# Fused linear attention and SwiGLU block on one core: fewer waits at the end, a last block in three pieces, and a reordered head

## The chip, the cores and the metric

One core of one Trainium2 chip. The metric is device time in microseconds (us) of one execution. The profiled executions have a span about 1.8 us below the time of the same run, so spans are compared with spans and times with times.

## The reference, cut to what matters

```python
def reference(A_x, A_wqkv, A_wo, B_x, B_w_gate, B_w_up, B_w_down):   # x: 1 x 2048 x 1024, F = 3584
    x = A_x
    xn = _layernorm(x, axis=-1)
    s = _A_ref(xn, A_wqkv, A_wo)             # linear attention, 32 heads, phi(t) = elu(t) + 1
    g = _silu(_B_ref(xn, B_w_gate, B_w_up, B_w_down))   # SwiGLU feed-forward, then silu
    return x + s * g
```

Everything starts from layer-normed x, so the first products need x tiles (128 tokens x 1024), their normalisation, their transposes, and the first blocks of `wqkv`. The last thing computed is a block of the down projection, which then goes through silu, a multiply, a transpose, the residual add and a store.

## The kernel before

The kernel builds a list of operations with data dependencies, runs a list scheduler 24 times with estimated durations, keeps the best order, and emits one fixed instruction stream for each engine with semaphore waits between them. The products use Strassen-Winograd sums. Four parts matter.

The waits. Each emitted operation knows what its engine has already waited for, directly or through others (`ek`):

```python
    def emit(self, esem):
        ...
            for p in sorted(o.preds, key=lambda p: -pos[p]):
                ...
                sem, key, val, ek = p.ev
                if kn.get(key, 0) >= val:
                    continue
                prog[o.eng].append(("w", sem, val))
                for k, v in ek.items():
                    if kn.get(k, 0) < v:
                        kn[k] = v
        ...
        self.count = count
...
        prog = PL.emit(esem)
        for s in semn.values():                       # at the end: SyncE waits for every DMA semaphore
            if id(s) in PL.count:
                prog["sp"].append(("w", s, PL.count[id(s)]))
```

The warm-up, the loads and the normalisation of the head (NWARM = 14):

```python
        dve([], [wz_r], lambda h: h.memset(wz, 0.0), 256)
        for n in range(NWARM):
            b = n % 8
            pe_mm([ident_r, wz_r], [bank_r[b]], [(ps[b][:, :], ident[:, :], wz, True, True)])
...
        def x_load(i):
            ...
            if i:
                dma([], [s.r], s.ap(), xf[i * 128:(i + 1) * 128, :], dsem("x%d" % s.k), 256 * KB).urgent = 10.0
                return
            for h, e in enumerate(("sp", "act")):     # tile 0 in two halves, on SyncE's and ScalarE's queue
                ...
        def wkv_load(w, j, k):                        # one block of wqkv, 512 KB
            ...
        for n, (fn, args) in enumerate(((x_load, (0,)), (wkv_load, (0, 1, 0)), (x_load, (1,)), (wkv_load, (0, 1, 1)),
                                        (wkv_load, (0, 0, 0)), (wkv_load, (0, 0, 1)), (x_load, (2,)),
        ...
        ln_tile(0)
        t_tile(0)          # transposes of tile 0 on TensorE
        ln_tile(1)
        p_piece(0, 0, 1)   # products of tile 0 with blocks 1 and 2
        p_piece(0, 0, 0)   # products of tile 0 with blocks 3 and 4
        t_tile(1)
        p_piece(1, 0, 1)
        ...
```

The end of the last down block: 14 pairs of products for each half of 256 tokens, then silu, multiply, transposes, add, and a store of 128 KB; between them the 256 KB store of an earlier block (`self.turn0`):

```python
                for h, b in enumerate((self.sets[1].b, self.b2)):
                    for n in range(0, NPAIR, 2):
                        ...
                        if turns and n == 2:
                            self.turn0()
                        if turns and n == 8:
                            turn(turns.pop())
                    ... # Silu, multiply
                    turns.append(h)
                turn(1)
```

## Time and profile before

| | before |
|---|---|
| time, median of 3 runs | 718.42 us (717.95 to 718.52) |
| span of the profiled execution | 716.4 us |
| TensorE busy | 99% of the span |
| first product at the steady rate (13th product) | 11.34 us |
| fourth block of wqkv landed | 11.29 us |
| last store issued, landed | 712.35, 714.35 us |

PE is TensorE, DVE is VectorE, ACT is ScalarE, SP is SyncE; L275 is the line of the helper that issues matmuls, L418 that of a tensor-tensor helper, so go by the tiles. First the top of the profile's page, which gives span and busy time of each engine:

```profile
span 716.4 us, 11259 instructions
PE 706.9 (99%) x4114; PEld 389.3 (54%) x4128; DVE 641.5 (90%) x1530; ACT 405.1 (57%) x777; POOL 12.4 (2%) x35
```

Next the view by windows: for each stretch its length, then the busy time of each engine, the clock granted to TensorE (1.00 is full), the DMA share and GB/s.

```profile
6.36:11.34 4.98, 4.19 (x29) 1.91 (x29) 3.69 (x9) 2.00 (x6) 0.55 (x1) 1.00 1.07 367
11.34:711.00 699.66, 697.51 (x4070) 385.37 (x4084) 634.66 (x1513) 401.50 (x771) 8.30 (x14) 1.00 0.48 135
...
714.40:716.50 2.10, 0.00 (x0) 0.00 (x0) 0.00 (x0) 0.00 (x0) 0.00 (x0) 0.72 0.02 4
```

From 11.34 to 711 us TensorE is busy 697.5 of 699.7 us: only the ends can give time. In the last 2.1 us no engine computes anything.

The head in TensorE's timeline (start, length from first start to last end, then the group; in brackets the idle time before it and what ended it):

```profile
7.11 1.04 PE L275 MATMUL ps<-H,X 128*128 128x512 bf16 x4
8.45 1.02 PE L275 MATMUL ps<-H,X 128*128 128x512 bf16 x4 [0.30 <-DMA H<-in_A_wqkv_dram]
9.85 1.04 PE L275 MATMUL ps<-H,X 128*128 128x512 bf16 x4 [0.38 <-DMA H<-in_A_wqkv_dram]
10.73 0.61 PE L282 MATMUL ps<-ident,W 128*128 128x128 f16 x8
11.34 1.69 PE L275 MATMUL ps<-H,X 128*128 128x512 bf16 x7
```

Three groups of four products with blocks 1, 2 and 3. The first waits for the evacuated transposes of tile 0 (block 1 had landed at 4.92); the second and third begin as their block lands (8.31 and 9.81). Then come the eight transposes of tile 1, and then the 13th product, the first with block 4. The 13th product starts at 11.34, right behind the transposes. But a load is done when all 16 of its parts have landed, and in the trace's record of landings the last part of block 4 comes at 11.29 (the first at 9.85). The transposes are hidden in a wait for a load.

The same stretch on VectorE (tile 1's variance, a sum of weights, tile 1's normalise):

```profile
8.02 0.15 DVE L740 TENSOR_SCALAR veps<-mv 128x1 f32<-128x1 f32 x1
8.34 0.69 DVE L418 TENSOR_TENSOR H<-H 128x1024 f16<-128x1024 bf16 x1 [0.16 <-DMA H<-in_A_wqkv_dram]
8.95 0.73 DVE L750 TENSOR_SCALAR W<-W,mv,rstd 128x512 f16<-128x512 bf16 x2
```

The tail: SyncE's semaphore waits at the end (by source line: count, length in ns, first and last start).

```profile
L267 SPq EVENT_SEMAPHORE  x48: 28/28/28, 712.8 to 716.0; - x48
```

And SyncE's timeline, where L421 is the helper that issues DMAs:

```profile
707.18 5.54 SPq L421 DMA_DIRECT2D out_dram<-TM  x5
```

48 closing waits, each for two semaphores, run at one per 0.06 us (a count of 49, as in the prediction, includes one of the barrier that follows). The five stores were issued at 707.18 (256 KB), 710.19 (256), 710.82 (128), 711.24 (256) and 712.35 (128); the last landed at 714.35.

### The profile page before, as it was taken

What the parts mean: (1) busy time and instruction counts of PE and PEld (TensorE: products, weight loads), DVE (VectorE), ACT (ScalarE), POOL (GpSimd) and SP (SyncE); (2) the same over time, 40 slices, a digit from 0 to 9 for tenths busy, and PEclk for the clock granted to TensorE, in tenths of its full rate; (3) what the DMA queues carried; (4) which work ended last, traced back from release to release, by engine and by line L of the source; (5) the groups of instructions that cost most, each with busy time, mean ns of one, the idle gap of its engine ahead of it and who ended that gap; (6) DMA issues with size and microseconds to landing.
All of it is one profiled execution on the core that took longest, in us unless ns stands there. A gap on an engine that the chain in (4) does not pass through costs nothing.

```text
span 716.4 us, 11259 instructions
## 1 busy us (share of the span) xinstructions
PE 706.9 (99%) x4114; PEld 389.3 (54%) x4128; DVE 641.5 (90%) x1530; ACT 405.1 (57%) x777; POOL 12.4 (2%) x35
## 2 busy tenths in 40 slices
PE   8999999999999999999999999999999999999997
PEld 3544445555555555555556455555555555565653
DVE  7999988989999999998957999999999999797852
ACT  3677644887679565664212157766876756521111
POOL 2111000000000000000000000000000000000000
PEclk9999999999999999999999999999999999999999
DMA  9426235245464343326496954132716241747653
GB/s 307 104 60 131 47 117 177 67 146 186 153 188 128 111 155 110 112 64 179 133 198 171 269 155 133 60 118 93 205 59 192 74 147 64 197 115 171 138 157 86
DMA packets 138743, 98.12 MB, mean 137 GB/s; under 512 B 32832, under 2 KB 135744, under 8 KB 138688
## 3 DMA queue, kind: packets, MB, share of 16 engines
q1 hardware_dynamic: 138544, 97.28, 47.7%
q8 instruction: 32, 0.52, 0.3%
q10 hardware_dynamic: 144, 0.13, 0.1%
q14 instruction: 23, 0.19, 0.1%
HBM read 77.59 MB, written 12.71 MB: 126 GB/s over the span
## 4 chain that ended last, share of the span: by engine, by line
PE 94%; DVE 3%; DMA 1%; ACT 1%; issue 0%; SPq 0%; DVEq 0%
PE ps L275 94%; DMA H<-in_A_wqkv_dram 1%; DVE W L418 1%; DVE H L418 1%; DVE ps L418 1%; ACT TM L407 0%; PE ps L282 0%; DVE P L418 0%; DVE TM L418 0%; SPq L421 0%; DVE H L811 0%; ACT ps L407 0%; ACT H L407 0%; DVE TM L810 0%; SPq L717 0%
## 5 line engine op out<-in xcount | busy, mean ns | idle before, releaser
L275 PE MATMUL ps<-X,W 128*128 128x512 f16 (+1 forms) x1358 | 289.1, 352 | 0.7 <-DVE W L418 0.6
L407 ACT ACTIVATE TM<-ps 128x512 f16<-128x512 f32 (+2 forms) x354 | 186.6, 549 | 109.1 <-PE ps L275 106.8
L275 PE MATMUL ps<-H,W 128*128 128x512 f16 (+2 forms) x1090 | 218.8, 351 | 0.9 <-DVE ps L418 0.4
L418 DVE TENSOR_TENSOR W<-W 128x1024 f16<-128x1024 bf16 (+5 forms) x416 | 186.2, 482 | 5.4 <-PE ps L275 4.7
L275 PEld LDWEIGHTS ps<-X,W 128*128 128x128 f16 (+1 forms) x1358 | 132.1, 98 | 105.1 <-DVE W L418 1.1
L275 PEld LDWEIGHTS ps<-H,W 128*128 128x128 f16 (+1 forms) x1096 | 105.6, 98 | 95.0 <-DVE ps L418 1.5
L418 DVE TENSOR_TENSOR ps<-ps,TM 128x256 f32<-128x256 f32 (+1 forms) x250 | 131.3, 528 | 13.3 <-PE ps L275 10.9
L407 ACT ACTIVATE ps<-ps 128x512 f32<-128x512 f32 (+1 forms) x173 | 85.0, 492 | 100.1 <-PE ps L275 98.3
L275 PE MATMUL ps<-P,W 128*128 128x256 f16 (+1 forms) x516 | 99.5, 319 | 0.0
L407 ACT ACTIVATE H<-ps 128x512 f16<-128x512 f32 (+1 forms) x126 | 75.1, 605 | 41.5 <-PE ps L275 41.3
L418 DVE TENSOR_TENSOR H<-H 128x1024 f16<-128x1024 f16 (+5 forms) x126 | 70.7, 579 | 0.6 <-ACT H L407 0.2
L275 PEld LDWEIGHTS ps<-P,W 128*128 128x128 f16 (+1 forms) x516 | 50.2, 98 | 29.5 <-DVE ps L418 0.7
L407 ACT ACTIVATE TM<-TM 128x512 f16<-128x512 f32 (+1 forms) x61 | 38.0, 622 | 47.0 <-DVE TM L418 46.8
L275 PE MATMUL ps<-W 128*128 128x256 f16 (+1 forms) x330 | 62.0, 282 | 0.2
L418 DVE TENSOR_TENSOR TM<-ps,TM 128x512 f32<-128x512 f32 (+2 forms) x62 | 41.5, 670 | 13.5 <-PE ps L275 12.4
L418 DVE TENSOR_TENSOR H<-H,TM 128x512 f16<-128x512 f16 x112 | 45.5, 418 | 8.9 <-ACT H L407 8.7
L275 PEld LDWEIGHTS ps<-W 128*128 128x128 f16 (+1 forms) x330 | 31.6, 98 | 32.5 <-DVE ps L418 1.3
L275 PE MATMUL ps<-H,X 128*128 128x512 bf16 (+1 forms) x147 | 35.0, 379 | 0.9 <-DMA H<-in_A_wqkv_dram 0.7
L275 PE MATMUL ps<-H,P 128*128 128x512 bf16 (+1 forms) x108 | 26.4, 379 | 0.1
L418 DVE TENSOR_TENSOR H<-ps,TM 128x512 f16<-128x512 f32 (+1 forms) x35 | 24.0, 686 | 1.9 <-PE ps L275 1.5
L275 PEld LDWEIGHTS ps<-H,X 128*128 128x128 f16 (+1 forms) x150 | 14.0, 98 | 17.9 <-ACT X L407 1.2
L418 DVE TENSOR_TENSOR TM<-TM,W 128x512 f16<-128x512 f16 (+1 forms) x39 | 14.1, 365 | 10.5 <-ACT TM L407 10.5
(96 smaller groups left out, 430.2 us busy)
## 6 DMA issues: line engine op xcount, KB each, us to landing
W<-in_B_w_gate_dram SPq DMA_DIRECT2D x14, 1024.0 KB, 5.1
W<-in_B_w_up_dram SPq DMA_DIRECT2D x13, 1024.0 KB, 5.5
W<-in_B_w_down_dram SPq DMA_DIRECT2D x14, 896.0 KB, 6.4
H<-in_A_wqkv_dram SPq DMA_DIRECT2D x8, 512.0 KB, 8.1
H<-r_scratch SPq DMA_DIRECT2D x32, 128.0 KB, 3.7
W<-m_scratch SPq DMA_DIRECT2D x4, 1024.0 KB, 5.1
s_scratch<-TM SPq DMA_DIRECT2D x32, 128.0 KB, 2.6
TM<-in_A_x_dram SPq DMA_DIRECT2D x16, 256.0 KB, 3.2
```

The lines of the kernel that those rows point to most:

```text
L275: last = h.matmul(o, l, r, start=st, stop=sp, skip_group_check=True)
L407: q = PL.op("act", reads, writes, lambda h: h.activation(o, i, func, **kw), nel(o) / (1000.0 if "bias" in kw or not isinstance(kw.get("sca ...
L418: return dve(reads, writes, lambda h: h.tensor_tensor(o, a, b, op), nel(o), 1.92 if fast else 0.96)
```

## The change

The intent: await at the end only the DMAs that SyncE does not already know to be complete; shorten the closing chain by cutting the last block into pieces of 256, 128 and 128 tokens, the last stored from ScalarE's queue; start the warm-up of TensorE earlier and with fewer full-size products; and load x tiles 0 and 1 ahead of all weights, so that tile 1 is normalised sooner.

```diff
@@ emit
-        self.count = count
+        for o in (o for o in self.order if o.sem is not None):
+            sem, key, val, _ = o.ev
+            if val == count[key] and know["sp"].get(key, 0) < val:
+                prog["sp"].append(("w", sem, val))
@@ warm-up (NWARM 14 -> 15)
-        wz_r = TM.reg(0, 1 * KB)
-        dve([], [wz_r], lambda h: h.memset(wz, 0.0), 256)
+        wz_r = [TM.reg(0, KB // 4), TM.reg(KB // 4, 3 * KB // 4)]
+        dve([], [wz_r[0]], lambda h: h.memset(wz[:, 0:128], 0.0), 64)
+        dve([], [wz_r[1]], lambda h: h.memset(wz[:, 128:512], 0.0), 192)
         for n in range(NWARM):
             b = n % 8
-            pe_mm([ident_r, wz_r], [bank_r[b]], [(ps[b][:, :], ident[:, :], wz, True, True)])
+            m = 512 if n > 3 else 128
+            pe_mm(wz_r[:1 + n // 4], [bank_r[b]], [(ps[b][:, 0:m], wz[:, 0:128], wz[:, 0:m], True, True)])
@@ ln_tile: tile 1's second statistics half now waits for tile 0's last normalise
             if i == 1:
-                for o in (oA, oB):
-                    o.preds.add(first_var[0])
-                    first_var[0].succs.append(o)
+                for o, q in zip((oA, oB), first):
+                    o.preds.add(q)
+                    q.succs.append(o)
@@ loads
-        for n, (fn, args) in enumerate(((x_load, (0,)), (wkv_load, (0, 1, 0)), (x_load, (1,)), (wkv_load, (0, 1, 1)),
+        for n, (fn, args) in enumerate(((x_load, (0,)), (x_load, (1,)), (wkv_load, (0, 1, 0)), (wkv_load, (0, 1, 1)),
@@ last down block
+                        self.last = [(0, 256, b), (256, 128, balloc()), (384, 128, balloc())]
...
+                    PL.op("act" if h == 2 else "sp", [vr], [], lambda h: h.dma_start(dst, v), 0.47,
+                          sem=dsem("oz%d" % h), nbytes=512 * n)
...                                     # the loop over two halves becomes a loop over self.last
-                        if turns and n == 2:
+                        if h == 1 and n == 2:
                             self.turn0()
-                        if turns and n == 8:
+                        if turns and n == (4 if h == 2 else 10):
                             turn(turns.pop())
...
-                turn(1)
+                for h in reversed(turns):
+                    turn(h)
@@ end of build_kernel
         prog = PL.emit(esem)
-        for s in semn.values():
-            if id(s) in PL.count:
-                prog["sp"].append(("w", s, PL.count[id(s)]))
```

More of the change, by code (lines that the diff above doesn't have):

```diff
@@ L283, in _tr_group, with build_kernel @@
     return last
-def build_kernel(nc, A_x, A_wqkv, A_wo, B_w_gate, B_w_up, B_w_down, out, WINDOW=6, NWARM=14, NPE=4, LEAD=12.0):
+def build_kernel(nc, A_x, A_wqkv, A_wo, B_w_gate, B_w_up, B_w_down, out, WINDOW=6, NWARM=15, NPE=4, LEAD=12.0):
     S, D, FF = 2048, 1024, 3584
@@ L725, in build_kernel @@
         xnslot = {}
-        first_var = []
+        first = []
         def ln_tile(i):
@@ L741, in ln_tile @@
             if i == 0:
-                first_var.append(o0)
+                first.append(o0)
             pool([ver, nh_r], [rsr], lambda h: h.tensor_tensor(rstd[:, j, :], veps[:, j, :], neg_half[:, :], ALU.pow), 0.56)
@@ L749, in ln_tile @@
                 for c in range(0, 1024, n):
-                    dve([s.r, mvr, rsr], [o.sub(2 * c, 2 * n).r], lambda h, c=c: h.tensor_scalar(
+                    o0 = dve([s.r, mvr, rsr], [o.sub(2 * c, 2 * n).r], lambda h, c=c: h.tensor_scalar(
                         oa[:, c:c + n], xa[:, c:c + n], mv[:, j, 0:1], rstd[:, j, :], ALU.subtract, ALU.mult), n, 2.6)
+                if i == 0:
+                    first.append(o0)
             else:
@@ L1462, in do @@
                         b = self.sets[1].b
-                        self.b2 = balloc()
-                        act([bank_r[b]], [bank_r[self.b2], bank_r[b]], ps[self.b2][:, 0:256], ps[b][:, 256:512], ACT.Identity)
+                        self.last = [(0, 256, b), (256, 128, balloc()), (384, 128, balloc())]
+                        for o, n, q in self.last[1:]:
+                            act([bank_r[b]], [bank_r[q], bank_r[b]], ps[q][:, 0:n], ps[b][:, o:o + n], ACT.Identity)
                     tick()
@@ L1481, in turn @@
                 def turn(h):
-                    gh = g.sub(h * KB // 2, KB // 2)
+                    o, n, _ = self.last[h]
+                    t0, m = o // 128, n // 128
+                    gh = g.sub(2 * o, 2 * n)
                     b = balloc_part()
-                    pb = ps[b][:, 0:128].bitcast(FP16).rearrange("p (m n) -> p m n", n=128)
-                    pe_tr([gh.r, ident_r], [bank_r[b]], [(pb[:, m, :], gh.ap(FP16)[:, m * 128:(m + 1) * 128],
-                                                          ident[:, :]) for m in range(2)])
@@ L1487, in turn @@
-                    v = xv[:, 2 * h:2 * h + 2, :]
-                    vr = q.sub(h * KB, KB).r
-                    tt([bank_r[b], vr], [vr], v[:, :, 128:256], pb, v[:, :, 128:256], ALU.add)
-                    row = p * 1024 + h * 256
-                    dma([vr], [], of[row:row + 256, c * 256:(c + 1) * 256].rearrange("(m p) n -> p m n", p=128), v,
-                        dsem("oz%d" % h), 128 * KB)
-                for h, b in enumerate((self.sets[1].b, self.b2)):
+                    pb = ps[b][:, 0:n // 2].bitcast(FP16).rearrange("p (m n) -> p m n", n=128)
@@ new lines, in turn @@
+                    pe_tr([gh.r, ident_r], [bank_r[b]], [(pb[:, k, :], gh.ap(FP16)[:, k * 128:(k + 1) * 128],
+                                                          ident[:, :]) for k in range(m)])
+                    v = xv[:, t0:t0 + m, :]
+                    vr = q.sub(t0 * 512, m * 512).r
+                    tt([bank_r[b], vr], [vr], v[:, :, 128:256], pb, v[:, :, 128:256], ALU.add)
+                    row = p * 1024 + o
+                    dst = of[row:row + n, c * 256:(c + 1) * 256].rearrange("(m p) n -> p m n", p=128)
@@ L1495, in finish @@
+                    PL.op("act" if h == 2 else "sp", [vr], [], lambda h: h.dma_start(dst, v), 0.47,
+                          sem=dsem("oz%d" % h), nbytes=512 * n)
+                for h, (o, m, b) in enumerate(self.last):
                     for n in range(0, NPAIR, 2):
                         tv, tr = self.t4[n // 2]
-                        pe_mm([wr, tr], [bank_r[b]], [(ps[b][:, 0:256], wv[:, n + k, :],
-                                                       tv[:, k, 256 * h:256 * h + 256], False, n + k == NPAIR - 1)
-                                                      for k in range(2)])
@@ L1500, in finish @@
-                        if turns and n == 2:
+                        pe_mm([wr, tr], [bank_r[b]], [(ps[b][:, 0:m], wv[:, n + k, :], tv[:, k, o:o + m], False,
+                                                       n + k == NPAIR - 1) for k in range(2)])
+                        if h == 1 and n == 2:
                             self.turn0()
-                        if turns and n == 8:
+                        if turns and n == (4 if h == 2 else 10):
                             turn(turns.pop())
-                    gh, sh = g.sub(h * KB // 2, KB // 2), sf.sub(h * KB // 2, KB // 2)
@@ L1505, in finish @@
-                    act([bank_r[b]], [gh.r], gh.ap(FP16), ps[b][:, 0:256], ACT.Silu)
+                    gh, sh = g.sub(2 * o, 2 * m), sf.sub(2 * o, 2 * m)
+                    act([bank_r[b]], [gh.r], gh.ap(FP16), ps[b][:, 0:m], ACT.Silu)
                     tt([gh.r, sh.r], [gh.r], gh.ap(FP16), gh.ap(FP16), sh.ap(FP16), ALU.mult, True)
                     turns.append(h)
-                turn(1)
+                for h in reversed(turns):
+                    turn(h)
             def keep(self, w):
```

## The prediction

> **What bounds the kernel now.** TensorE. The page gives it 99% of a 716.4 us span; the 512-column matmuls in the middle of the timeline start every 0.216 us and the windows view has PE busy 697.5 of the 699.7 us between 11.34 and 711.0. The change does not touch that stretch, so only the two ends can give time.
>
> *Head (timeline, waits).* The warm-up products start at 1.41 us, when GpSimd's identity is ready, and end when tile 0's transposes start (6.36). Between 6.36 and 11.34 PE has real gaps: it waits for loads of wqkv at 8.45 (the load landed 8.31) and 9.85 (landed 9.81), start-to-start 0.68 and 0.76 us instead of 0.22, and tile 1's transposes (about 0.45 us) run only at 10.73, after those gaps.
>
> *Tail (timeline of SyncE, and the waits' line by source).* The last matmul ends about 710.9; Silu 0.38, multiply 0.29, transposes 0.28, add 0.29 us follow, the last store is issued at 712.35 and lands 2.0 us later, at 714.35. SyncE meanwhile starts 49 semaphore waits, one every 0.06 us, two semaphores each, from 712.77 to 716.02; about 1.6 us of them come after the last landing. They end the program, not the store. Closing barrier: 0.4 us.
>
> **What the change does.**
>
> 1. *Waits.* Only the last stores of the output remain unknown to SyncE (every load and scratch store has been waited for by somebody it has waited for): I expect 4 to 9 waits, nearly all done before the last landing. The end becomes last landing + about 0.5 us, against 2.07 us now. Worth about 1.5 us, all on the critical path.
>
> 2. *Three pieces.* PE work is equal (14x256 columns at 0.109 us become 28x128 at about 0.056, an estimate from the transposes' spacing). The closing chain gets shorter by about 0.3 us (128-column Silu, multiply, add; one transpose). But the profile shows the DMA engines over 90% busy at about 290 GB/s (512 B packets) from 711.1 to 713.95: the last four stores, 768 KB, are a backlog which the change does not shrink. The Trainium skill ("DMA: Bandwidth & Descriptors", Issuing engines are not separate DMA queues) says queues of different engines share the same 16 DMA engines; so issuing the last piece from ScalarE saves only issue time. I expect the last landing to move by only 0.1 us (0 to 0.4).
>
> 3. *Head.* x tile 1 lands about 1 us earlier; half of its statistics (0.69 us) fits in VectorE's idle 0.68 us while GpSimd computes tile 0's rstd. Tile 1 is normalised near 8.3 instead of 8.95, so its transposes fit into the gap before 9.85. About 0.6 us of PE idle time is filled, and everything after shifts earlier. Warm-up products starting 0.3 us earlier are worth nothing themselves: tile 0's transposes wait for LayerNorm. The same page set ("TensorE: Matmul & The Clock Gate", What's actually happening) has a busy window of about 3.4 us before full clock; here spacing falls from 0.427 to 0.216 us at 5.3 us, after 3.9 us. I expect that to hold.
>
> Sum: 1.5 + 0.1 + 0.6 = 2.2 us.
>
> **Predicted 716.2 us (715.5 to 717.1).** Faster by over 2%: 0.5%; within 2%: 99%; slower: 0.5%.
>
> **Right or wrong by.** Waits: SyncE's waits after the last store number under ten; span end minus last landing near 0.5 us. Pieces: last landing minus last full 512-column matmul changes under 0.4 us. Head: transposes of tile 1 before 9.9 us, and the matmuls that start at 11.34 start near 10.7.
>
> **What would make it wrong.** The schedule is recomputed: a different order in the middle could cost or give some 0.3 us. The wqkv loads, delayed by x tile 1, could land later. The large store could be put behind the small ones, lengthening the backlog.

## More of the kernel before

An order that is decided on estimates is then executed as it stands: an instruction that waits holds up all that stand behind it on its engine (the result shows a case, with its times).

In the head the DMA engines are busy throughout (share 1.07).

## The result, and the profile after

| | before | after |
|---|---|---|
| time, median of 4 runs each | 718.47 us (717.95 to 719.32) | 717.4 us (716.78 to 718.21) |
| ratio | | 0.9985, interval 0.9967 to 1.0002 |
| span of the profiled execution | 716.4 us | 716.5 us |

A ratio is the mean time of one kernel's fast runs over that of the other's of the same rounds, so it is not quite the ratio of the medians quoted. Each run of an experiment has its own runs of the kernel before beside it on the same chip. The median fell by about 1.1 us, half of the 2.2 us expected, to just outside the range; the interval of this one comparison just includes no change at all, so the gain itself rests on the groups of runs and the traces below.

The profiled execution of after has the same span as that of before, though its timed runs are faster. So the span has to be cut into segments, which is easy in this kernel, because TensorE is busy almost without a break in the middle:

| segment of the profiled execution, us | before | after |
|---|---|---|
| start to the 40th product | 17.39 | 18.95 |
| 40th to the last 512-column product | 689.74 | 689.71 |
| last 512-column product to the last landing | 7.22 | 7.32 |
| last landing to the end | 2.10 | 0.48 |
| sum | 716.45 | 716.46 |

The closing waits gained 1.62 us, the head lost 1.56, and the stretch before the last landing lost 0.10. Windows of after, cut like those of before:

```profile
6.58:12.91 6.33, 5.43 (x28) 2.40 (x29) 3.26 (x8) 1.83 (x6) 0.93 (x1) 0.73 1.06 353
12.91:712.50 699.59, 697.54 (x4088) 385.73 (x4099) 634.11 (x1514) 402.16 (x772) 8.31 (x14) 1.00 0.48 134
...
716.00:716.50 0.50, 0.00 (x0) 0.00 (x0) 0.00 (x0) 0.00 (x0) 0.00 (x0) 0.50 0.00 0
```

The middle is unchanged (697.5 us busy), the last stretch fell from 2.1 to 0.5 us, and the head grew from 4.98 to 6.33 us at a mean clock of 0.73. TensorE's timeline in the head:

```profile
6.58 0.71 PE L285 MATMUL ps<-ident,W 128*128 128x128 f16 x8 [0.86 <-DVE W L755]
8.19 4.44 PE L278 MATMUL ps<-H,X 128*128 128x512 bf16 x12 [0.90 <-ACT X L410]
12.46 0.61 PE L285 MATMUL ps<-ident,W 128*128 128x128 f16 x8
12.91 1.46 PE L278 MATMUL ps<-H,X 128*128 128x512 bf16 x6
```

The order on TensorE is what it was: eight transposes, twelve products, eight transposes of tile 1, then the rest. Tile 1's transposes start at 12.46 us, later than before and not earlier. The first product begins at 8.19 rather than 7.11: the bracket names ScalarE, but the evacuation it needs had ended at 7.28; the first block of wqkv landed at 8.06. VectorE shows why tile 1 is late too:

```profile
7.60 0.21 DVE L744 BATCH_NORM_AGGREGATE mv<-stats 128x2 f32<-128x12 f32 x1
9.53 0.69 DVE L421 TENSOR_TENSOR H<-H 128x1024 f16<-128x1024 bf16 x1 [1.72 <-DMA H<-in_A_wqkv_dram]
10.14 0.15 DVE L745 TENSOR_SCALAR veps<-mv 128x1 f32<-128x1 f32 x1
...
11.34 0.74 DVE L755 TENSOR_SCALAR W<-W,mv,rstd 128x512 f16<-128x512 bf16 x2 [0.45 <-POOL rstd L748]
```

The load of tile 1 has landed at 4.24 (5.76 in before), but its statistics are aggregated only at 7.60 (7.78 in before). The tiny next step (`veps`) stands in VectorE's fixed order behind a sum of weights, which waits 1.72 us for a load, so tile 1 is normalised at 11.34 instead of 8.95.

The clock, in the windows between the trace's own changes of the granted clock:

```profile
4.95:8.36 3.41, 1.65 (x13) 0.73 (x12) 2.69 (x8) 1.21 (x4) 0.56 (x1) 1.00 0.88 278
8.36:11.78 3.42, 3.42 (x9) 1.09 (x8) 1.80 (x5) 0.12 (x1) 0.93 (x1) 0.50 1.08 376
```

In one window of 3.41 us TensorE was busy 1.65 us, and the next window was granted half clock. In before the full clock held from 5.34 us on.

The tail: the waits, then the stores on SyncE's queue, then the one on ScalarE's.

```profile
L270 SPq EVENT_SEMAPHORE  x3: 17/27/28, 714.8 to 716.0; - x3
```

```profile
708.71 3.36 SPq L424 DMA_DIRECT2D out_dram<-TM  x2
712.38 0.90 SPq L1502 DMA_DIRECT2D out_dram<-TM  x2
713.32 0.45 SPq L424 DMA_DIRECT2D out_dram<-TM  x1
```

```profile
713.74 0.35 ACTq L1502 DMA_DIRECT2D out_dram<-TM  x1
```

Three waits are left besides the barrier's; the last starts at 716.0, as the last store lands. The two lines with L424 are the large stores (256 KB each), those with L1502 the pieces; the third large one is now issued at 713.32, behind the small ones of 128 and 64 KB at 712.38 and 712.79. It landed at 715.74, and the last landing, at 715.99, is that of the 64 KB piece on ScalarE's queue, issued behind it at 713.74.

### The profile page after: what moved, and what is told of

Same layout as the page of the kernel before. It is cut to its first block, busy times and chain, and to the rows that moved or that the text cites. A ratio compares the mean times of both kernels' runs of the same rounds, so it can differ in the third digit from the quotient of the medians.

```text
span 716.5 us, 11250 instructions
## 1 busy us (share of the span) xinstructions
PE 707.9 (99%) x4129; PEld 390.1 (54%) x4143; DVE 641.3 (90%) x1533; ACT 405.6 (57%) x779; POOL 12.8 (2%) x35
## 4 chain that ended last, share of the span: by engine, by line
PE 95%; DVE 3%; ACT 1%; DMA 0%; issue 0%; DVEq 0%
PE ps L278 95%; DVE W L421 1%; DVE H L421 1%; DVE ps L421 1%; ACT TM L410 0%; DMA W<-in_A_x_dram 0%; PE ps L285 0%; DVE H L818 0%; DVE stats L738 0%; ACT X L410 0%; ACT ps L410 0%; ACT H L410 0%; DVE TM L421 0%; DVE TM L817 0%; DVE stats L739 0%
## 5 line engine op out<-in xcount | busy, mean ns | idle before, releaser
L278 PE MATMUL ps<-X,W 128*128 128x512 f16 (+2 forms) x1372 | 289.2, 350 | 0.6 <-DVE W L421 0.6
L410 ACT ACTIVATE TM<-ps 128x512 f16<-128x512 f32 (+3 forms) x355 | 186.8, 548 | 110.6 <-PE ps L278 108.2
L421 DVE TENSOR_TENSOR ps<-ps,TM 128x256 f32<-128x256 f32 (+1 forms) x250 | 130.7, 525 | 13.4 <-PE ps L278 10.9
L421 DVE TENSOR_TENSOR TM<-ps,TM 128x512 f32<-128x512 f32 (+3 forms) x63 | 41.5, 660 | 13.2 <-PE ps L278 12.4
```

What stands on the lines that cost most here:

```text
L278: last = h.matmul(o, l, r, start=st, stop=sp, skip_group_check=True)
L410: q = PL.op("act", reads, writes, lambda h: h.activation(o, i, func, **kw), nel(o) / (1000.0 if "bias" in kw or not isinstance(kw.get("sca ...
L421: return dve(reads, writes, lambda h: h.tensor_tensor(o, a, b, op), nel(o), 1.92 if fast else 0.96)
```

## The experiments

Eighteen runs on several chips. All results were correct except the four named as wrong. The theories:

- *Head theory (load)*: the head ends when block 4 of wqkv lands, and loading x tile 1 ahead of the weights on SyncE's queue makes it land later.
- *Rival: warm-up theory (clock)*: the new warm-up leaves TensorE too idle, so the clock falls to half and the head gets longer.
- *Rival: middle theory*: the recomputed order, or a stall near 404 us that differs from run to run, eats the gain.
- *Tail theory*: the three pieces with the large store behind the small ones cost what the waits gained.

The segments of every trace, with the landing of the last part of block 4 and the long stall near 404 us, are in one table. `mid` is 40th product to last 512-column product, `tail` from there to the last landing, `close` from there to the end.

| kernel | time, median us | ratio to before | block 4 landed | 40th product | mid | tail | close | stall |
|---|---|---|---|---|---|---|---|---|
| before | 718.47 | | 11.29 | 17.39 | 689.74 | 7.22 | 2.10 | 0.63 |
| after | 717.4 | 0.9985 | 12.49 | 18.95 | 689.71 | 7.32 | 0.48 | 0.63 |
| e1_again | 718.19 | 0.9995 | 11.62 | 17.72 | 689.76 | 7.34 | 0.48 | 0.63 |
| e2_waits | 716.74 | 0.9977 | 11.70 | 17.80 | 689.75 | 7.21 | 0.49 | 0.63 |
| e3_oldloads | 716.72 | 0.9981 | 12.16 | 18.26 | 690.86 | 7.33 | 0.48 | 1.68 |
| e4_oldwarm | 716.94 | 0.9984 | 11.46 | 17.55 | 689.76 | 7.33 | 0.49 | 0.63 |
| e5_look | 717.79 (1 run) | | 11.62 | 17.50 | 690.74 | 7.33 | 0.49 | 1.42 |
| e6_longwarm | 717.25 | 0.9986 | 11.82 | 17.70 | 689.99 | 7.34 | 0.49 | 0.68 |
| e7_shortwarm | 718.18 | 0.9995 | 11.13 | 18.10 | 689.94 | 7.33 | 0.48 | 0.63 |
| e8_tile1 | 719.03 | 1.0006 | 12.36 | 17.98 | 691.64 | 7.33 | 0.48 | 0.93 |
| g_before | 718.24 | 0.9999 | 10.90 | 16.78 | 689.95 | 7.21 | 2.11 | 0.63 |
| g_after | 716.87 | 0.9977 | 12.40 | 18.28 | 689.96 | 7.33 | 0.48 | 0.63 |
| g_waits | 717.03 | 0.9974 | 11.51 | 17.39 | 690.46 | 7.21 | 0.49 | 1.15 |
| g_oldwarm | 717.6 | 0.9982 | 12.22 | 18.10 | 689.96 | 7.32 | 0.48 | 0.63 |
| t_after | 716.58 | 0.9973 | 11.69 | 17.57 | 689.96 | 6.65 | 0.48 | 0.63 |
| t_oldloads | 716.24 | 0.9968 | 11.06 | 16.95 | 689.95 | 6.63 | 0.48 | 0.63 |
| t_bothold | 716.61 | 0.9971 | 11.19 | 17.07 | 690.70 | 6.64 | 0.48 | 1.38 |
| u_after_actx1 | 716.03 | 0.9967 | 10.51 | 16.53 | 689.96 | 7.32 | 0.49 | 0.63 |
| u_before_actx1 | 718.27 | 0.9997 | 10.95 | 17.05 | 689.94 | 7.22 | 2.14 | 0.63 |
| t_actx1 | 715.59 | 0.9957 | 10.55 | 16.50 | 690.40 | 6.64 | 0.49 | 1.10 |

Each row has five timed runs, except before and after (4 each), e8_tile1 (4) and e5_look (1). The interval of each ratio is about 0.0013 either way, some 0.9 us. That is too wide to tell most single rows apart, so what is said below of steps under 1 us rests on groups of rows and on segments.

A caution for the columns `40th product` and `mid`: in the traces of before, after and e1_again to e4_oldwarm the record of one product ahead of the 40th is missing (in before at 12.86 us its weight load is recorded, the product is not, and two starts stand 0.43 us apart instead of 0.22). What is counted as the 40th is the 41st product in these six, so 0.22 us stand in the head that in the other traces stand in `mid`.

### e1_again: the changed kernel once more, unaltered

No edit; it asks how much of after's profile was that one execution.

> The changed kernel once more, unaltered. Clock theory (fewer warm-up columns let TensorE's clock fall to half for one stretch of 3.4 us in some runs): times fall in two groups, near 716.8 and near 718, and the slow ones that were due to the clock list a mean clock of about 0.997. Load theory (x tile 1 ahead of the first wqkv block makes that block land late): times vary with that landing, at a mean clock of 1.0 too. Chance theory (the start of the transfers varies from run to run in both kernels): the kernel before varies as much, and the ratio to it settles near 0.998.

Measured 718.19 us (717.04 to 718.5), ratio 0.9995 (0.9982 to 1.0007). Of the profiled execution, TensorE's timeline in the head and the window of the clock:

```profile
11.03 0.62 PE L285 MATMUL ps<-ident,W 128*128 128x128 f16 x8
11.66 1.47 PE L278 MATMUL ps<-H,X 128*128 128x512 bf16 x6
```

```profile
4.90:8.31 3.41, 2.44 (x16) 0.93 (x14) 2.78 (x8) 1.21 (x4) 0.56 (x1) 1.00 1.00 295
8.31:11.72 3.41, 2.68 (x18) 1.22 (x18) 2.13 (x6) 0.87 (x2) 0.93 (x1) 1.00 1.08 367
```

Here the clock held (2.44 us busy in the window), block 4 landed at 11.62 and the span was 715.3. So the fall of the clock belongs to single executions, not to the kernel as such, and after's first profile was one of its worse heads. Even in the good one tile 1's transposes start at 11.03, not before 9.9. Taken together, the two sets of runs of the unaltered changed kernel (0.9985 and 0.9995) put its gain nearer 0.7 us than 1.1.

### e2_waits: only the waits

```diff
 (before)
-        self.count = count
+        for o in (o for o in self.order if o.sem is not None):
+            ... # as in after
@@
-        for s in semn.values(): ...
```

> The kernel before with nothing but the shorter list of waits at the end. Prediction and all theories: about 1.5 us less than before (ratio 0.9979), span end minus last landing about 0.5 us, head as before (first product at 7.1 us).

Measured 716.74 us, ratio 0.9977 (0.9964 to 0.9989), which is -1.65 us of 718.5; `close` fell from 2.10 to 0.49. The waits alone give as much as or more than the whole change. So the other parts together gave nothing, or cost something.

### e3_oldloads and e4_oldwarm: the change without its load order, and without its warm-up

```diff
 (after, e3_oldloads)
-                for o, q in zip((oA, oB), first):
-                    o.preds.add(q) ...
+                for o in (oA, oB):
+                    o.preds.add(first[0]) ...
-        ... ((x_load, (0,)), (x_load, (1,)), (wkv_load, (0, 1, 0)), ...
+        ... ((x_load, (0,)), (wkv_load, (0, 1, 0)), (x_load, (1,)), ...
```

> The changed kernel with the old order of the first loads and the old dependency of tile 1's statistics; new warm-up kept. Load theory: first wqkv block lands near 4.9 us, first product near 7.1 us, no slow group, median 716.3 to 716.7. Clock theory: warm-up products still end at 5.3 us, so the clock can still fall, runs near 718 at clock 0.997 remain.

Measured 716.72 us, four runs at 716.4 to 716.79 and the profiled one at 718.66, which had the long stall near 404 us; ratio 0.9981 (0.9969 to 0.9994).

```diff
 (after, e4_oldwarm)
-... NWARM=15 ...
+... NWARM=14 ...
-            m = 512 if n > 3 else 128
-            pe_mm(wz_r[:1 + n // 4], [bank_r[b]], [(ps[b][:, 0:m], wz[:, 0:128], wz[:, 0:m], True, True)])
+            pe_mm([ident_r, wz_r], [bank_r[b]], [(ps[b][:, :], ident[:, :], wz, True, True)])
```

> The changed kernel with the old warm-up (14 products of 512 columns, starting at 1.4 us and ending at 6.3 us); new load order kept. Clock theory: no run with a mean clock of 0.997, median near 716.8 with no group near 718. Load theory: as the changed kernel, first product only when the delayed first wqkv block has landed (8 us).

Measured 716.94 us, ratio 0.9984 (0.9971 to 0.9998). Both ratios lie within the interval of the other: this pair did not tell the rivals apart by time. In both traces `tail` is 7.33, so the pieces cost 0.1 us and no more; that ends the tail theory as a cause of a loss.

### e5_look: a third look at the changed kernel

> The changed kernel again, for one more trace. In the traces so far the 13th product starts 0.04 us after the fourth wqkv block has landed, unless TensorE is at half clock. If the run is slow (about 718), clock theory: products start 0.427 us apart for part of the head, whatever the mean clock listed. Load theory: products are 0.216 us apart and wait for transfers that landed late.

One run, 717.79 us, state unknown. The head is as in e1_again (40th product at 17.50). What is long is `mid`. TensorE's timeline of before near 404 us has this line:

```profile
403.76 1.47 PE L275 MATMUL ps<-H,W 128*128 128x512 f16 x6 [0.36 <-DVE ps L418]
```

and that of e5_look this one:

```profile
404.87 1.47 PE L278 MATMUL ps<-H,W 128*128 128x512 f16 x6 [1.15 <-DVE ps L421]
```

TensorE sat idle 1.15 us instead of 0.36 at the same place in the program. This stall is 0.63 us from start to start in most traces, and 1.10 to 1.68 in five (e3_oldloads, e5_look, g_waits, t_bothold, t_actx1), with old and with new head. One of those, g_waits, differs from before only in the closing waits and in smaller stores. So the stall varies between executions, and is not a thing that the changed order brought.

### e6_longwarm and e7_shortwarm: more and less warm-up

```diff
 (after, e6_longwarm)                     (e3_oldloads, e7_shortwarm)
-NWARM=15                                 -NWARM=15
+NWARM=20                                 +NWARM=7
```

> The changed kernel with 20 warm-up products in place of 15 (five more of 512 columns); every other instruction and its order the same. Clock theory: TensorE stays busy up to tile 0's transposes, the slow group near 718.2 goes away, median 716.6 to 716.9. Load theory: the first wqkv block lands as late as before, so the slow group stays and the median is near 718.

Measured 717.25 us, ratio 0.9986 (0.9972 to 1.0): as after's 0.9985. A longer warm-up buys nothing that these runs can resolve.

> The kernel of the old load order (e3_oldloads) with the warm-up cut to 7 products (four of 128, three of 512 columns, ending near 2.8 us); nothing else differs. Clock theory: most products of the head run at half clock, twelve of them alone cost 2.5 us against about 1 us of waiting that is there anyway; nearly all runs slow, median 718 to 719. Load theory: as e3_oldloads, 716.7.

Measured 718.18 us, ratio 0.9995 (0.9983 to 1.0008), against 0.9981 for the same kernel with 15. In the trace the full clock comes only at 11.39 us. TensorE's timeline:

```profile
7.14 4.85 PE L278 MATMUL ps<-H,X 128*128 128x512 bf16 x12
...
12.27 1.03 PE L278 MATMUL ps<-H,X 128*128 128x512 bf16 x4
```

Block 4 landed at 11.13, early, but the 13th product starts 1.14 us after it, for the twelve before it ran at half clock until the very end. In the other traces it starts 0.04 to 0.19 us after the landing, but for after's first profile (0.42, half clock) and e8_tile1. So a fall of the clock is real and costs about 1 us when it is forced; with the change's warm-up as written it appears in one trace of the changed kernel in three. e4_oldwarm, g_oldwarm and t_bothold, all with the old warm-up, are not measurably faster than their partners with the new one. The clock is a minor part of what is missing.

### e8_tile1: make the predicted step happen

This kernel has the old warm-up, and forces what the prediction took for granted: tile 1 is normalised before the sums of weights, its transposes stand after eight products, and their evacuation stands before the first exponential.

```diff
 (e4_oldwarm)
-        p_piece(0, 0, 1)
-        p_piece(0, 0, 0)
         t_tile(1)
+        p_piece(0, 0, 1)
         p_piece(1, 0, 1)
+        p_piece(0, 0, 0)
@@
-        combos(KVV[0])
+        combos(KVV[0], first[-1])     # the sums of weights wait for tile 1's normalise
@@ first exponential
+            if turned and turned[-1] not in o.preds:
+                o.preds.add(turned[-1]) ...
```

> The changed kernel with the old warm-up, and with tile 1 forced to the place that the prediction gave it: its normalisation ahead of the weights' sums on VectorE, its transposes after 8 products instead of 12, its evacuation ahead of the first Exp. If the prediction's 0.6 us was lost only because the planner left tile 1 where it was: the 13th product starts about 0.6 us sooner after the fourth wqkv block's landing (before it), and the time is 716.3, against 716.9 of e4_oldwarm. Rival (the gain is given back, since VectorE then has the weights' sums later): the 40th product is no earlier than in e4_oldwarm (17.55 us), time 716.9 or more.

Measured 719.03 us (4 runs, 718.6 to 719.18), ratio 1.0006 (0.9992 to 1.002), slower than every other form of the change. TensorE's timeline:

```profile
10.28 0.61 PE L285 MATMUL ps<-ident,W 128*128 128x128 f16 x8
10.91 3.41 PE L278 MATMUL ps<-H,X 128*128 128x512 bf16 x15
```

Tile 1 is normalised at 8.58, the transposes move to 10.28, and tile 1's products no longer wait for block 4: the 40th product comes 5.62 us after the landing, instead of 5.88 in the traces that miss no record (e4_oldwarm's 6.09 counts one product more). That is a gain of 0.26 us, under half of the 0.6 predicted. But block 4 landed at 12.36 in this trace, and `mid` grew to 691.64, with longer steps between starts, among others 0.58 us up to 14.7 and 0.82 us up to 29.7 us. The trace puts the wait at 14.7 down to VectorE and that at 29.7 to ScalarE; that the sums which were pushed back are behind them was not traced. What the head gained was given back, and more. In this schedule the predicted step, forced in this way, was not free.

### g_before, g_after, g_waits, g_oldwarm: less output traffic before the middle

To test the middle theory, the output stores of the first half of the tokens were cut to a quarter, with a wrong result (rows of the output stay unwritten). If they cause the stall near 404 us, the spread should shrink.

```diff
                     if len(seen) == 2:
-                        dma([q.r], [], of[row:row + 512, ...
+                        n = 1 if p == 0 else 4
+                        dma([q.r], [], of[row:row + n * 128, ...
```

> The kernel before, storing only a quarter of the first half's output (wrong result on purpose), which takes 3 MB off the transfers of the first pass, among them those around 386 to 402 us, where traces show a wait of TensorE of 0.63 us in most runs and 1.4 to 1.7 us in two slow ones. Middle theory (the groups near +1.2 us of every kernel come from transfers landing late there): the stall at 404 shrinks in the trace, and the runs lie within 0.6 us of each other. Clock or load theory of the head: the spread of about 2 us that the kernel before shows stays.

Measured 718.24 us, ratio 0.9999 (0.9985 to 1.0013).

> The changed kernel with the same quarter stores. Middle theory: no slow group, runs within 0.6 us, and 1.3 to 1.6 us below g_before (waits 1.6, pieces -0.1, head 0). Clock theory: two groups 1.2 us apart remain, median less than 1 us below g_before. As predicted at first: 2.2 us below g_before.

Measured 716.87 us, ratio 0.9977 (0.9965 to 0.999), five runs from 716.01 to 717.86.

> The kernel before with the shorter list of waits alone, and quarter stores. All theories: 1.5 to 1.6 us below g_before. The distance to g_after is what head and pieces do together: 0.1 to 0.2 us by the middle theory (g_after slower), more than 0.5 us by the clock theory.

Measured 717.03 us, ratio 0.9974 (0.9962 to 0.9987), stall 1.15 in its trace.

> The changed kernel with the old warm-up and quarter stores. Clock theory: 0.5 us or more below g_after, without its slow runs. Middle theory: as g_after within 0.3 us.

Measured 717.6 us, ratio 0.9982 (0.997 to 0.9995).

The spread did not shrink (1.1 to 1.9 us from fastest to slowest of five), and the stall still reached 1.15 us. So cutting these stores to a quarter does not remove it, and its cause remains open. As the middle is not altered otherwise, the four serve as further samples of the head: with the old load order block 4 landed at 10.90 and 11.51, with the new one at 12.40 and 12.22.

### t_after, t_oldloads, t_bothold: the large store issued early

The planner was told that the DMA transposes of the last pass land about 2.5 us after issue. It then plans the large store before the small ones. The only edit is to an estimate:

```diff
 (after, t_after)
-                          sem=dsem("tp%d" % o.k), nbytes=200 * KB)
+                          sem=dsem("tp%d" % o.k),
+                          nbytes=-440e3 if (p, self.h) == (1, 1) else 200 * KB)
```

t_oldloads is t_after with the load order of before (the edit of e3_oldloads), t_bothold is t_oldloads with the old warm-up as well.

> The changed kernel; the planner is told that the last down pass's DMA transposes land 2.5 us after their issue (as traces show) instead of 4.4, so that the last large store is issued about 2 us sooner, before the small ones. Backlog theory of the tail: last landing minus last 512-column product falls from 7.33 to about 6.85 us. Rival (the closing chain or the store's own 2 us bind): it stays within 0.1 of 7.33. Head as in the other traces of the new load order: fourth wqkv block lands near 12.0 us.

Measured 716.58 us, ratio 0.9973 (0.9961 to 0.9986). SyncE's stores:

```profile
707.24 3.67 SPq L424 DMA_DIRECT2D out_dram<-TM  x3
711.25 0.90 SPq L1502 DMA_DIRECT2D out_dram<-TM  x2
```

All three large stores are now issued before the small ones, and `tail` falls to 6.65: 0.57 us less than before, 0.68 less than after. So the last landing comes half a microsecond earlier than in before, once the backlog ends with little data. How much of that is due to the three pieces is not shown: no run issued the large store early without them.

> As t_after with the old load order, new warm-up kept. Load theory: fourth wqkv block near 11.45 us, about 2590 KB moved by 10 us against 2400, 0.5 us less than t_after in time. Warm-up theory: as t_after within 0.2 us.

Measured 716.24 us, ratio 0.9968 (0.9955 to 0.998).

> As t_oldloads with the old warm-up too, so the kernel before in the head, and waits, three pieces and the early large store in the tail. Load theory: as t_oldloads within 0.2 us, about 716.3. Warm-up theory: 0.5 us below t_oldloads.

Measured 716.61 us, ratio 0.9971 (0.9958 to 0.9983). With e3_oldloads against after, this is the second time that the old load order comes out ahead of the new by a little (0.9981 against 0.9985, 0.9968 and 0.9971 against 0.9973), each time within the noise: by time alone the order of the loads is not told apart. The landings say it more plainly:

| where x tile 1 is loaded | traces | block 4: first part landed | last part landed, mean (standard deviation) |
|---|---|---|---|
| SyncE's queue, behind block 1 (old order) | 8 | 9.87 | 11.37 (0.41) |
| SyncE's queue, ahead of block 1 (new order) | 9 | 10.20 | 11.96 (0.40) |
| ScalarE's queue (next section) | 3 | 10.05 | 10.67 (0.24) |

The difference of the first two rows is 0.59 us with a standard error of 0.20. The bytes moved agree: by 10 us it was 2526 to 2749 KB in the eight traces of the first row, 2363 to 2548 in the nine of the second, 2683 to 2747 in the three of the third. The means of the first two, 2659 and 2460, lie 200 KB apart, which at some 360 GB/s takes 0.6 us (an estimate). The new order widens the spread from first to last part from 1.5 to 1.8 us.

### u_after_actx1, u_before_actx1, t_actx1: tile 1 on the other queue

If the load of tile 1 in SyncE's queue delays the blocks, issuing it from ScalarE's queue, where otherwise only half of tile 0 goes, should bring them forward.

```diff
             xslot[i] = s
+            if i == 1:
+                PL.op("act", [], [s.r], lambda h: h.dma_start(s.ap(), xf[128:256, :]), 0.47, sem=dsem("x%d" % s.k),
+                      nbytes=256 * KB)
+                return
```

> The changed kernel with x tile 1 issued from ScalarE's queue and nothing else altered. Queue theory (tile 1 in SyncE's queue puts the DMA engines out of step, and TensorE waits for the slowest part of the fourth wqkv block): parts of that block land within 0.4 us of each other, last near 10.6 us; median 716.2, ratio 0.9968, so 1.2 us below the changed kernel's pooled 717.4 to 718.2. Rival (t_actx1 was a lucky run): 717 to 718 as before.

Measured 716.03 us (715.91 to 717.12), ratio 0.9967 (0.9953 to 0.9981). TensorE's timeline:

```profile
7.52 2.76 PE L278 MATMUL ps<-H,X 128*128 128x512 bf16 x12
10.14 0.72 PE L285 MATMUL ps<-ident,W 128*128 128x128 f16 x8
10.70 2.54 PE L278 MATMUL ps<-H,X 128*128 128x512 bf16 x11
```

The twelve products run without a gap, block 4 landed at 10.51, and the 13th product starts at 10.70, where the prediction had it. The view by windows shows where the earlier data came from. The stretch from 5 to 7 us in before:

```profile
5.00:7.00 2.00, 2.00 (x15) 0.96 (x12) 1.32 (x4) 0.33 (x2) 0.56 (x1) 1.00 0.87 284
```

in after:

```profile
5.00:7.00 2.00, 1.14 (x10) 0.43 (x9) 1.86 (x6) 0.10 (x1) 0.56 (x1) 1.00 0.80 244
```

and in u_after_actx1:

```profile
5.00:7.00 2.00, 0.57 (x6) 0.23 (x4) 1.59 (x5) 0.00 (x0) 0.56 (x1) 1.00 1.06 369
```

Between 5 and 7 us the DMA engines move 284, 244 and 369 GB/s (means by row of the table above: 295, 257 and 367). The difference of after and u_after_actx1, 125 GB/s over 2 us, is 250 KB, which at the later rate of some 360 GB/s takes 0.7 us; the last part of block 4 came 1.98 us sooner, and the rest is that its parts landed 0.6 us apart instead of 2.8. An obvious rival is issue time, since with tile 1 gone from its queue SyncE issues block 4 at 2.80 instead of 3.29 (3.30 in before). It does not explain the gain: 0.49 us is less than the 1.29 between the means of the last two rows, the first part of block 4 lands hardly sooner (10.05 against 10.20), and before and after, which issue block 4 at the same time, differ too.

> The kernel before with x tile 1 issued from ScalarE's queue and nothing else altered (the planner's own estimate for it is 0.5 us longer, since the order shifts a little). Queue theory: fourth block's last part near 10.6 us instead of 11.4, 0.3 to 0.9 us below before (ratio 0.9988 to 0.9996). Rival: ratio 1.000, last part near 11.4 us.

Measured 718.27 us, ratio 0.9997 (0.9984 to 1.0009): block 4 at 10.95, 40th product at 17.05. Both fall short of what was expected (10.6, and a ratio of 0.9988 to 0.9996), and the interval leaves open whether there is a gain. In the trace the 40th product is only 0.12 us earlier than in before, with the missing record allowed for: of the 0.34 us that block 4 came sooner, 0.2 were lost in a new gap at 13.4 us.

> As t_after, with x tile 1 issued from ScalarE's queue, so that the wqkv blocks stand in SyncE's queue 0.5 us sooner. If the delay comes from the blocks standing behind tile 1 in one queue: fourth block near 11.4 us, 2590 KB by 10 us. If it comes from tile 1's bytes moving that early at all: near 12.0 us, 2400 KB, as t_after.

This is t_after with the same edit. Measured 715.59 us, all five runs from 715.35 to 715.91, ratio 0.9957 (0.9944 to 0.9971), even though its trace has the longer stall (1.10). It beats both kernels, by 3.0 us of medians against its own runs of before (718.56), and by about 1.8 against after, whose runs are of another round.

### The segments add up

Add up, for each kind of kernel, what its traces show against before: the waits -1.62; `tail` +0.11, or -0.57 with the large store early; block 4 by the means of its load order, +0.59 or -0.70. The sums are made after the fact from the same traces, but the times are separate runs. The measured column is the ratio, turned into us of 718.5.

| kernels | waits | tail | block 4 | sum | measured |
|---|---|---|---|---|---|
| e2_waits | -1.62 | 0 | 0 | -1.6 | -1.7 |
| after, e1_again, e4_oldwarm, e6_longwarm, g_after, g_oldwarm (mean ratio 0.9985) | -1.62 | +0.11 | +0.59 | -0.9 | -1.1 |
| e3_oldloads | -1.62 | +0.11 | 0 | -1.5 | -1.4 |
| t_after | -1.62 | -0.57 | +0.59 | -1.6 | -1.9 |
| t_oldloads, t_bothold | -1.62 | -0.57 | 0 | -2.2 | -2.3, -2.1 |
| u_after_actx1 | -1.62 | +0.11 | -0.70 | -2.2 | -2.4 |
| u_before_actx1 | 0 | 0 | -0.70 | -0.7 | -0.2 |
| t_actx1 | -1.62 | -0.57 | -0.70 | -2.9 | -3.1 |

The sums follow the measured order with differences of at most 0.5 us, inside the interval of a row. g_before (0 by the sum, -0.1 measured) and g_waits (-1.6, -1.9) fit too; e7_shortwarm and e8_tile1 stand outside, for the reasons shown in their sections, and e5_look has no ratio. For u_before_actx1 the mean of the landings promises more than its own trace shows (0.12 us).

## Why the prediction was right or wrong

**The waits: right.** Predicted -1.5 us, with 4 to 9 waits and span end minus last landing near 0.5 us. Measured: 3 closing waits, fewer than predicted, 0.48 us, -1.62 us in the traces, -1.65 by time alone (e2_waits). The Trainium skill ("Advanced Engine Details and Errata", Network/Comms) gives 50 to 100 ns for reading a semaphore's value from a sequencer; the trace's one satisfied wait per 0.06 us lies in that range.

**Three pieces: near.** Predicted a last landing earlier by 0.1 us (0 to 0.4); measured 0.1 us later, 7.21 or 7.22 became 7.32 to 7.34 in every trace with the pieces in which the large store goes last. The named risk, "the large store could be put behind the small ones", came true; t_after shows what it cost by taking it away (7.32 to 6.65).

**Head: wrong, and this is the step that failed.** The prediction said: "Tile 1 is normalised near 8.3 instead of 8.95, so its transposes fit into the gap before 9.85. About 0.6 us of PE idle time is filled, and everything after shifts earlier." The step has two parts, that tile 1 would run sooner because its load lands sooner, and that running its transposes sooner would save TensorE time. Three things stand in its place.

First, none of it happened beyond the earlier landing (4.24 instead of 5.76). Normalise started at 11.34 in after's trace and 10.46 in e1_again's, transposes at 12.46 and 11.03. The prediction reasoned as if an engine ran what was ready. But the order is fixed in advance on estimates: TensorE kept tile 1's transposes behind the twelve products, and VectorE got a sum of weights, which waits for a load, ahead of tile 1's variance.

Second, the transposes that were to be moved cost nothing in before. The 13th product starts 0.04 to 0.05 us after block 4 lands there, so they were inside a wait. To gain, later products would have to overtake that wait; e8_tile1 forced it, gained 0.26 us by the 40th product, and lost more in new gaps behind.

Third, the head ends with block 4, and the change delays block 4: 11.37 to 11.96 us on average. This was listed among what would make the prediction wrong ("the wqkv loads, delayed by x tile 1, could land later") and given no weight in the sum. So the term was -0.6 and by the landings is about +0.6. That shift of 1.2 us is about the whole difference between 716.2 and 717.4; that the two fit so well is partly luck, since the same kernel run again gave 718.19. Times alone do not resolve what the order of the loads costs (e3_oldloads 0.9981 against 0.9985), the landings and the bytes moved do. Moving that single load to the other queue gave 716.03 us, with the 13th product at 10.70 (u_after_actx1).

The prediction leaned on the Trainium skill ("DMA: Bandwidth & Descriptors", Issuing engines are not separate DMA queues), by which issuing on several engines only saves the sequencer's time to initiate a DMA. For the tail nothing here speaks against that. For the head the measurement differs, and it decides: after and u_after_actx1 differ only in the queue of one 256 KB load. That saved 0.49 us of issue time, but block 4 landed 1.29 us sooner in the mean of the traces, and the DMA engines moved 369 instead of 244 GB/s from 5 to 7 us.

**The clock: "I expect that to hold" was mostly right.** In one of the three traces of the unaltered changed kernel it fell to half for 3.41 us, and the 40th product came 6.46 us after the landing instead of 6.10, so about 0.4 us there. "TensorE: Matmul & The Clock Gate" (What's actually happening) describes a free-running window of 3413 ns; the trace agrees with changes at 4.95, 8.36 and 11.78 us. As a cause for the median this rival falls: kernels with old, new and longer warm-up have ratios of 0.9984, 0.9985 to 0.9995 and 0.9986.

**Open.** Why a load of tile 1 ahead of the weights in SyncE's queue leaves the DMA engines less full from 5 to 7 us is not shown; only that it does, and that the other queue avoids it. One thing in the traces goes with it: the next load behind block 4 (x tile 2) took SyncE 0.50 to 0.62 us to issue in the eight traces of the old order, 1.40 to 2.98 us in the nine of the new, and 0.75 to 1.29 us with tile 1 on ScalarE's queue. Whether this is a cause or a consequence was not tested. What lengthens the stall near 404 us in some executions is not known. The 0.0010 between the ratios of after and of e1_again, one and the same kernel, shows what such runs can resolve; not every timed run has a trace, so the longer ones among them are not all explained.

## What to carry to other kernels

Before costing a moved instruction, ask which wait ends last at that point, and compare the start of the next product with the landing of the load that it needs: work that ends just as a load lands is hidden, and moving it gains nothing. In a kernel with fixed instruction orders, a thing that becomes ready sooner does not run sooner unless the order says so (here a step that could start at 7.8 started at 10.14). And ask what a load that is moved forward does to those behind it in its queue: here they landed 0.6 us later. When times spread as much as the effect, cut the traces at a few common events and add up the segments.

## What the Trainium skill lacked or had wrong

- "DMA: Bandwidth & Descriptors", Issuing engines are not separate DMA queues, says that several issuing engines only save initiation time. Here moving one 256 KB load from SyncE's to ScalarE's queue saved 0.49 us of issue time, but raised the DMA rate between 5 and 7 us from 244 to 369 GB/s, and the fourth 512 KB block landed at 10.67 us (mean of 3 traces) instead of 11.96 (9 traces).
- The same page has nothing on how far apart the parts of one load land. Here first and last part of a 512 KB block landed 1.5 to 1.8 us apart (means) with tile 1 on SyncE's queue, 0.6 us with it on ScalarE's.
- "TensorE: Matmul & The Clock Gate", What's actually happening, gives the window but not how busy it must be to keep full clock. Here 1.65 of 3.41 us busy, with no idle stretch over 0.9 us, was followed by half clock, and 1.94 (u_after_actx1) was followed by full clock.
- "Advanced Engine Details and Errata", Network/Comms, gives the time of a semaphore read but not what a chain of closing waits costs: 48 waits took 3.25 us here, 1.6 us of it after the last landing.
